# Last keys in a sigmoid attention kernel: products with v issued ahead of the next round's last scores

## Chip, cores and metric

One Trainium2 chip, one core of it. The metric is the device time of one execution in microseconds, as the median of several; lower is better.

## What is computed

Eight batches, twelve heads, 448 positions, head size 64, all in float32; the attention is followed by a feed-forward layer.

```python
scores = scale * np.matmul(q, k.transpose(0, 1, 3, 2)) - np.log(S)    # q, k, v: 8 x 12 x 448 x 64
attn = 1.0 / (1.0 + np.exp(-scores))                                  # a sigmoid, no sum over the keys
attn_out = np.matmul(attn, v)
x = attn_out.transpose(0, 2, 1, 3).reshape(B * S, H * D)              # 3584 x 768
h = x @ w_in                                                          # w_in 768 x 2048
out = np.maximum(0.01 * h, h) @ w_out                                 # w_out 2048 x 768
```

## The kernel before

The kernel has three stages: the attention, the first product of the feed-forward layer (accumulators named f) and the second (accumulators named a). The change touches the attention alone.

A pair is two heads of one batch; there are 48 pairs, and they are worked on two at a time (x and y) in 24 rounds. The 448 keys are cut into four pieces of 128, 128, 128 and 64. For the first three pieces, `scores` makes one score tile each: three products of 64 x 128 array tiles for each of the two heads, in float32 halves (tiles `qks`). The 64 last keys have a score tile of their own for both pairs together, which `last_scores` makes with 64 x 64 array tiles from the raw `qk` tiles, four matmuls, which the trace shows as eight. ScalarE turns every score tile into weights by a sigmoid (`attn`): those of the first pieces into tiles `s`, those of the last keys into room behind a pair's `v` tile, so the trace calls that sigmoid `v<-sc`.

The products with v accumulate in one PSUM tile `pv` for both pairs. `attn_v` adds the first three pieces with 128 x 64 array tiles (twelve instructions a pair), `last_v` adds the last keys with 64 x 64 array tiles (eight instructions). `last_v` reads weights that were made one round earlier: the last scores of a round are computed at the end of the round before it. `Block.keep` then copies `pv` into an `x` tile, on ScalarE, and VectorE adds such tiles up and stores them.

A round is five slots, whose work stands in the list `works` (line 727): both pairs' scores, both pairs' `attn_v`, and `ending`. All matmuls, activations, copies and VectorE operations are pinned to the order in which the code issues them on their engine. ScalarE's order around the boundary of two rounds is therefore: the sigmoid of the last scores (issued within `ending`), the copy `keep` (put at the head of the next slot by `last_v`, with `first=True`), then six sigmoids of the next round's score tiles, in the order x 0, x 1, x 2, y 0, y 1, y 2, then the casts of later inputs.

PSUM is filled by one pool of four buffers (line 688). A round takes eight tiles from it: six score tiles, `pv` and the last scores. A new tile gets the free buffer whose last reader stands earliest in the program. So, in a round: tile x 2 takes the buffer of the last scores (read by the sigmoid `v<-sc`), y 0 that of the round before's `pv` (read by the copy), y 1 that of x 0, y 2 that of x 1, `pv` that of x 2, and the next last scores that of y 0; x 0 and x 1 take those of y 1 and y 2 of the round before. A tile's first weight load waits until the buffer's last reader is done.

Round 0 differs in the order of its first slots, and the last round has no last scores to make: its `last_v` follows `attn_v` directly.

Of the kernel before, what the change touches and what calls it, by code (L numbers as in the profile page):

```python
# [121 lines left out]
def attn_ffn_kernel(ctx: ExitStack, tc: tile.TileContext, qk, v, w_in, w_out, out):  # L122
# [570 lines left out]

    def ending(x, y):

        if y is not None:
            y.last_scores()
        x.last_v()

    unread = psum("s", "unread")[:, 0]  # L700
    for _ in range(IDLE):
# [8 lines left out]
    def when(p, i, jj=0):  # L710
        return base + 2 * (len(PRODUCTS1) * p + i) + jj

    own = {}
    for p in range(NQ):
        for i, n in enumerate(XS):
            if n in XS[:i]:
                continue
            x, t = Own(p, n), when(p, i)
# [6 lines left out]
    for r in range(rounds):  # L725
        x, y, *more = pairs[2 * r:2 * r + 6]
        works = [lambda: whole(x), lambda: whole(y), x.attn_v, y.attn_v, lambda: ending(y, more[0] if more else None)]
        if r == 0:

            works = [works[2], works[1], lambda: None, *works[3:]]  # L730
        if more:
            z, w = more[:2]
            later(0, z.load_v)
            later(1, w.load_v)
            later(2, z.high)
            later(3, z.low, w.high)
            later(4, w.low)
        for n, far in enumerate(more[2:]):
            later(1 + 3 * n, far.load_qk)
        for n, work in enumerate(works):  # L740
            slot(work)
            prepare(ROOM[n] * (r > 0))
# [25 lines left out]
    for g in range(SPLIT1, len(GROUPS1)):  # L768
        for j in range(KQ):
            x = w1[g, j] = Wide(g, j, wb, "wb")  # L770
            prepared_by(base + (g - SPLIT1) * 8 + j, x, 0)
    ws = {}
    for p in range(NQ):
        for n, load in STREAM.items():
            x = ws[p, n] = Streamed(p, n)
# [388 lines left out]
```

## Time and profile before

| what | value |
|---|---|
| median of three runs | 1016.13 us (1015.11 to 1016.46) |
| the profiled execution | 1016.21 us, of which span 1014.4 us |
| TensorE matmul busy | 1008.4 us, 99% of the span |
| VectorE busy | 852.1 us, 84% |
| ScalarE busy | 586.3 us, 58% |
| DMA | 288 GB/s in the mean |

The profile is of one execution. Busy times are those of instructions on an engine; the weight loads of TensorE (PEld) run beside its matmuls. The end of a matmul is a model's value, so a matmul that is shown busy need not be at its peak. A row's "idle before" names what ended an engine's wait, by the semaphore that came last.

### The profile page before, as it was taken

How to read it: one execution, taken by the hardware profiler on the slowest of the kernel's cores; microseconds unless marked ns; L12 is line 12 of the kernel's file. 1: busy time of each engine (PE TensorE's matmuls, PEld its weight loads, DVE VectorE, ACT ScalarE, POOL GpSimd, SP SyncE). 2: the span in 40 equal slices, each digit the busy share in tenths (PEclk: the TensorE clock that was granted, in tenths of full speed). 3: DMA queues.
4: the chain of work that ended last, by engine and by line, in shares of the span. 5: the costliest groups of instructions: out<-in, count | busy, mean ns of one | idle time of the engine just before them, and what ended most of it. 6: DMA issues, size and time to landing. Idle time of an engine off the chain costs nothing.

```text
span 1014.4 us, 15194 instructions
## 1 busy us (share of the span) xinstructions
PE 1008.4 (99%) x5642; PEld 844.0 (83%) x5642; DVE 852.1 (84%) x1116; ACT 586.3 (58%) x710; POOL 0.3 (0%) x5
## 2 busy tenths in 40 slices
PE   9999999999999999999999999999999999999998
PEld 5545555555999999999999999999999999999998
DVE  5888888887898789779788577799998999999886
ACT  7888888887645444445453665465453446645431
POOL 0000000000000000000000000000000000000000
PEclk9999999999999999999999999999999999999999
DMA  9899999997988897899797959996649897775633
GB/s 326 268 339 367 303 371 325 366 333 274 380 303 264 328 326 270 268 356 296 251 328 254 344 197 389 367 327 207 239 145 318 317 384 243 254 259 160 239 110 109
DMA packets 142025, 291.79 MB, mean 288 GB/s; under 512 B 11136, under 2 KB 71680, under 8 KB 141952
## 3 DMA queue, kind: packets, MB, share of 16 engines
q1 hardware_dynamic: 141088, 290.02, 81.9%
q8 instruction: 44, 0.72, 0.3%
q10 hardware_dynamic: 864, 0.80, 0.2%
q14 instruction: 29, 0.24, 0.1%
HBM read 189.33 MB, written 101.45 MB: 287 GB/s over the span
## 4 chain that ended last, share of the span: by engine, by line
PE 92%; DMA 3%; DVE 2%; issue 1%; ACT 1%; SPq 0%; ACTq 0%; DVEq 0%
PE f L159 34%; PE a L159 33%; PE pv L159 13%; PE sc L159 11%; DMA g<-h 1%; DMA g<-g 1%; DMA w<-t 1%; DMA g_m<-g 1%; DVE wd L159 1%; PE e_z L159 0%; DVE h L159 0%; DVE g L159 0%; DVE g_v L159 0%; PE e_a L159 0%; DVE g_m L159 0%
## 5 line engine op out<-in xcount | busy, mean ns | idle before, releaser
L159 PE MATMUL a<-gh,w 128*128 128x448 f32 x1224 | 345.9, 363 | 0.4 <-ACT o L159 0.4
L159 PE MATMUL f<-xh,w 128*128 128x448 f32 x960 | 272.5, 362 | 0.1
L159 PEld LDWEIGHTS a<-gh,w 128*128 128x128 f32 x1224 | 229.7, 188 | 15.6 <-ACT o L159 0.7
L159 PE MATMUL a<-gl,w 128*128 128x448 f32 x540 | 194.5, 360 | 0.4 <-DVE gl L159 0.4
L159 PEld LDWEIGHTS f<-xh,w 128*128 128x128 f32 x960 | 180.0, 187 | 12.8 <-issue 0.7
L159 PE MATMUL f<-xl,w 128*128 128x448 f32 x480 | 173.5, 361 | 0.0
L159 ACT CAST gh<-g 128x896 fp32r<-128x896 f32 x80 | 75.5, 943 | 124.7 <-DVE g L159 102.5
L159 DVE TENSOR_TENSOR h<-h,f 128x896 f32<-128x896 f32 x88 | 95.5, 1086 | 56.5 <-PE f L159 56.4
L159 ACT ACTIVATE s<-sc 128x896 f32<-128x896 f32 x144 | 119.8, 959 | 3.3 <-PE sc L159 3.3
L159 PE MATMUL pv<-s,v 128*64 128x448 f32 x576 | 113.8, 543 | 0.1
L159 PEld LDWEIGHTS a<-gl,w 128*128 128x128 f32 x540 | 101.0, 187 | 8.0 <-DVE gl L159 0.8
L159 ACT COPY h<-f 128x896 f32<-128x896 f32 x56 | 50.1, 909 | 97.4 <-PE f L159 73.7
L159 DVE TENSOR_TENSOR w<-w 128x768 fp32r<-128x768 f32 x112 | 104.3, 951 | 0.9 <-ACT w L159 0.9
L159 PEld LDWEIGHTS sc<-qks 64*128 64x128 f32 x876 | 79.5, 185 | 23.2 <-issue 16.9
L159 ACT CAST w<-w 128x768 fp32r<-128x768 f32 x112 | 92.9, 831 | 6.4 <-DMA w<-t 6.4
L159 PEld LDWEIGHTS f<-xl,w 128*128 128x128 f32 x480 | 90.0, 187 | 6.7
L159 PE MATMUL sc<-qks 64*128 64x448 f32 (+1 forms) x876 | 94.6, 366 | 0.1
L159 PE MATMUL f<-xh,ws 128*128 128x448 f32 x320 | 92.3, 363 | 0.6 <-DVE h L159 0.6
L159 PEld LDWEIGHTS pv<-s,v 128*64 128x64 f32 x576 | 39.2, 137 | 63.2 <-issue 54.0
L159 ACT ACTIVATE h<-h 128x896 f32<-128x896 f32 x56 | 53.2, 953 | 57.8 <-DVE h L159 57.5
L159 DVE TENSOR_TENSOR gl<-g,gh 128x896 fp32r<-128x896 f32 x72 | 78.1, 1085 | 4.4 <-ACT gh L159 3.7
L159 DVE TENSOR_TENSOR xl<-xl,xh 128x896 fp32r<-128x896 f32 x64 | 69.5, 1086 | 12.8 <-ACT xh L159 12.5
(79 smaller groups left out, 1058.7 us busy)
## 6 DMA issues: line engine op xcount, KB each, us to landing
w<-t SPq DMA_DIRECT2D x112, 384.0 KB, 5.1
g<-g SPq DMA_DIRECT2D x81, 448.0 KB, 5.8
xl<-xd SPq DMA_DIRECT2D x64, 448.0 KB, 6.5
g<-h SPq DMA_DIRECT2D x64, 448.0 KB, 5.6
qk<-in_qk SPq DMA_DIRECT2D x46, 448.0 KB, 5.7
xd<-x_s SPq DMA_DIRECT2D x36, 448.0 KB, 6.8
xd<-x SPq DMA_DIRECT2D x28, 448.0 KB, 6.6
wr<-in_w_in SPq DMA_DIRECT2D x24, 512.0 KB, 6.5
```

What stands on the lines that cost most here:

```text
L159: return lambda *args, **kw: tc.keep_in_program_order(issue(*args, **kw))
```

## The change

In `ending`, the two calls change places: y here is the first pair of the next round.

```diff
     def ending(x, y):
 
+        x.last_v()
         if y is not None:
             y.last_scores()
-        x.last_v()
```

No instruction, tile or transfer is added or removed. TensorE does the eight instructions of `last_v` first and then the eight of `last_scores`. On ScalarE the order stays as it was, the sigmoid of the last scores ahead of the copy of `pv`, since the copy is put into the next slot by either order. The order of the PSUM buffers stays too, since it goes by the last readers.

## Rows read from the trace of the kernel before

**Rows 1.** Busy time per engine in stretches; then granted clock, DMA share, GB/s.

```profile
core 0: us, PE busy (x) PEld busy (x) DVE busy (x) ACT busy (x) POOL busy (x), PEclk, DMA share, GB/s
0.00:4.00 4.00, 2.88 (x14) 2.53 (x14) 0.67 (x3) 1.85 (x3) 0.31 (x5) 1.00 0.49 130
...
16.00:250.00 234.00, 234.00 (x1747) 125.67 (x1744) 197.39 (x342) 197.25 (x262) 0.00 (x0) 1.00 0.93 328
250.00:1014.00 764.00, 759.58 (x3790) 709.67 (x3789) 649.56 (x765) 378.89 (x435) 0.00 (x0) 1.00 0.79 275
```

**Rows 2.** TensorE's matmuls in order of time: start us, us, what, count.

```profile
14.57 0.98 PE L159 MATMUL sc<-qk 64*64 64x448 f32 x8
15.37 0.93 PE L159 MATMUL pv<-v 64*64 64x448 f32 x8
16.23 3.91 PE L159 MATMUL sc<-qks 64*128 64x448 f32 x36
...
142.07 4.73 PE L159 MATMUL pv<-s,v 128*64 128x448 f32 x24
146.74 0.98 PE L159 MATMUL sc<-qk 64*64 64x448 f32 x8
147.54 0.93 PE L159 MATMUL pv<-v 64*64 64x448 f32 x8
148.40 3.91 PE L159 MATMUL sc<-qks 64*128 64x448 f32 x36
...
239.90 3.91 PE L159 MATMUL sc<-qks 64*128 64x448 f32 x36
243.74 4.73 PE L159 MATMUL pv<-s,v 128*64 128x448 f32 x24
248.40 0.98 PE L159 MATMUL pv<-v 64*64 64x448 f32 x8
```

**Rows 3.** The chain of waits that ended last, from 120 to 170 us.

```profile
by line: PE pv L159 54.1%; PE sc L159 45.9%
```

**Rows 4.** ScalarE, one instruction each, at the start of one round.

```profile
147.79 0.92 ACT L159 ACTIVATE v<-sc 128x896 f32<-128x896 f32 x1 [2.04 <-PE sc L159]
148.60 0.90 ACT L159 COPY x<-pv 128x896 f32<-128x896 f32 x1
149.39 0.94 ACT L159 ACTIVATE s<-sc 128x896 f32<-128x896 f32 x1
150.19 0.94 ACT L159 ACTIVATE s<-sc 128x896 f32<-128x896 f32 x1
150.99 0.96 ACT L159 ACTIVATE s<-sc 128x896 f32<-128x896 f32 x1
```

**Rows 5.** First weight loads of tiles x 2, y 0, y 1, y 2 and pv.

```profile
149.52 0.19 PEld L159 LDWEIGHTS sc<-qks 64*128 64x128 f32 x2
150.13 0.19 PEld L159 LDWEIGHTS sc<-qks 64*128 64x128 f32 x2
150.74 0.19 PEld L159 LDWEIGHTS sc<-qks 64*128 64x128 f32 x2
151.35 0.19 PEld L159 LDWEIGHTS sc<-qks 64*128 64x128 f32 x2
152.24 0.14 PEld L159 LDWEIGHTS pv<-s,v 128*64 128x64 f32 x2 [0.30 <-ACT s L159]
```

**Rows 6.** Weight loads and matmuls of the round's first score tile.

```profile
148.40 0.19 PEld L159 LDWEIGHTS sc<-qks 64*128 64x128 f32 x2 [0.71 <-issue]
148.51 0.19 PEld L159 LDWEIGHTS sc<-qks 64*128 64x128 f32 x2
...
148.40 0.47 PE L159 MATMUL sc<-qks 64*128 64x448 f32 x2
148.71 0.36 PE L159 MATMUL sc<-qks 64*128 64x448 f32 x2
148.91 0.36 PE L159 MATMUL sc<-qks 64*128 64x448 f32 x2
```

**Rows 7.** Round 0: sigmoids on ScalarE, and weight loads that wait for them.

```profile
11.88 0.91 ACT L159 ACTIVATE s<-sc 128x896 f32<-128x896 f32 x1
12.67 0.93 ACT L159 ACTIVATE s<-sc 128x896 f32<-128x896 f32 x1
...
12.84 0.14 PEld L159 LDWEIGHTS pv<-s,v 128*64 128x64 f32 x2 [0.48 <-ACT s L159]
13.65 0.14 PEld L159 LDWEIGHTS pv<-s,v 128*64 128x64 f32 x2 [0.54 <-ACT s L159]
```

**Rows 8.** ScalarE's sigmoids of the last scores, with the wait before each.

```profile
15.62 0.92 ACT L159 ACTIVATE v<-sc 128x896 f32<-128x896 f32 x1 [0.30 <-PE sc L159]
25.79 0.92 ACT L159 ACTIVATE v<-sc 128x896 f32<-128x896 f32 x1 [2.04 <-PE sc L159]
...
46.12 0.92 ACT L159 ACTIVATE v<-sc 128x896 f32<-128x896 f32 x1 [0.72 <-PE sc L159]
...
239.29 0.92 ACT L159 ACTIVATE v<-sc 128x896 f32<-128x896 f32 x1 [0.66 <-PE sc L159]
```

## Prediction

> **What bounds the kernel now.** I read the busy times by stretch first. Between 16 and 250 us, the attention, TensorE's matmuls cover 234.00 of 234.00 us, and behind it 759.58 of 764 [rows 1]; time is won or lost only where TensorE's stream gets shorter or gets a hole. The chain of waits in the middle of the attention runs through TensorE alone [rows 3]. The matmuls in order of time show a stream that repeats: scores, products with v, last scores, last products with v. From one round's scores to the next it takes 10.17 us, from 16.23 to 239.90 us in 22 such steps, which makes 23 rounds that begin behind an `ending` with last scores in it [rows 2]. The other engine to look at is ScalarE, which reads every score tile and so gives the PSUM buffers back. Over a whole round it has time left: the sigmoid of the last scores finds it idle each time, after 0.30 to 2.04 us of waiting for TensorE [rows 8]. But at the start of a round it works back to back, 0.80 us from start to start [rows 4], while TensorE makes a score tile in 0.61 us (149.52, 150.13, 150.74, 151.35) [rows 5]. For these 4 us ScalarE is the slower of the two, and TensorE runs on because four buffers stand between them. What is to be seen is how much of that lead is left at each tile.
>
> **What moves.** On TensorE the two blocks cost the same in either place. The eight instructions of the last scores begin at 146.74 us and the products 0.80 us later, and the round's scores follow 0.86 us behind [rows 2]. The last round has the products alone right behind `attn_v`, as the change puts them everywhere: they begin 4.66 us after `attn_v`, as the last scores do elsewhere, and take the same 0.98 us [rows 2]. So the new order needs no time of its own: the scores of the round would still begin at 148.40 us. No DMA is moved past another; SP's queue keeps its order, and its transfers start no earlier.
>
> What moves is the moment at which the last scores are ready: their end goes from 147.72 us (146.74 + 0.98) to 148.47 us (147.54 + 0.93), where the products end now. That is 0.75 us later [rows 2]. ScalarE waits for nothing else there [rows 4, 8], so the sigmoid of the last scores starts at 148.54 us in place of 147.79. The copy of `pv` stands behind it. Its data are ready 0.75 us earlier than before, and that is of no use: it is next in line and was already starting back to back. The six sigmoids stand behind the copy. Their scores were complete before they started, so they too are tied to ScalarE's own pace; all of this row of instructions goes 0.75 us later [rows 4].
>
> **Which weight load is late now.** A load that waited for ScalarE began 0.05 us after the sigmoid's end, twice: 11.88 + 0.91 to 12.84, and 12.67 + 0.93 to 13.65 [rows 7]. With that, and with the buffers' order:
>
> - Tile x 2 takes the last scores' buffer: free at 148.71 + 0.75 + 0.05 = 149.51 us, loaded at 149.52 [rows 4, 5]. Just in time. (Today it loads 0.02 us behind the copy's end at 149.50, too soon for a release by the copy; the trace agrees with the buffers' order.)
> - Tile y 0 takes `pv`'s: free at 149.50 + 0.80 = 150.30 us against 150.13: 0.17 late.
> - Tile y 1 takes that of x 0: free at 150.33 + 0.80 = 151.13 against 150.74.
> - Tile y 2 takes that of x 1: free at 151.13 + 0.80 = 151.93 against 151.35.
> - `pv` takes that of x 2: free at 151.95 + 0.80 = 152.75 against 152.24.
>
> What a late load costs lies between two bounds. A load runs beside the matmuls before it: behind an empty array the next load follows the first by 0.11 us, and the first matmul is recorded 0.11 us longer than the others (0.47 against 0.36), while two pairs of matmuls in the stream are 0.20 us apart [rows 6]. So a load can be late by some 0.10 us before its matmul is. With that cover the delays add up to 0.07 at y 0 (0.17 - 0.10), to 0.29 at y 1 (151.13 against 150.81, less 0.10), to 0.48 at y 2 (151.93 against 151.64, less 0.10), and at `pv`, where the load has no cover, to 0.51 (152.75 - 152.24). Without the cover they are 0.17, 0.39 and 0.58, and `pv` follows at 152.82. I take 0.51 us a round, since the first matmul's extra 0.11 us is the same thing seen from the other side, and keep 0.58 as the upper end. The lower end of this case is a release of 0.03 us in place of 0.05, which gives 0.49.
>
> **Is there slack at pv?** The profile gives `pv`'s load an idle time of 0.30 us that a sigmoid ended [rows 5]. But that sigmoid ended at 151.95 us [rows 4], and with 0.05 us it would have let the load go at 152.00. I take the wait until 152.24 to be TensorE's own: three changes of the array's tile size in a round, and the one at 248.40 in the last, all begin 0.06 to 0.07 us before the modelled end of the matmuls ahead (146.80, 148.47, 152.31 and 248.47) [rows 2], with ScalarE done or not. So 0.24 us of slack stand there, and the loss is 0.51 and not 0.75. The Trainium skill, TensorEngine Tiling (Array Packing), Tiling Modes, says that a change of the tiling mode, not of the tile alone, drains the array. By that rule the sum goes by 0.51; by the profile's label it would go by 0.75. The four places agree with the rule.
>
> Behind `pv`, the sigmoids of y are needed only 2 us and more into the products (12 of 24 instructions in 4.66 us) [rows 2], and are done by then. ScalarE's later casts lose nothing, as each round leaves it 0.30 us or more idle [rows 8] and the round gets longer. VectorE's sums of the copied tiles come 0.75 us later, and VectorE is busy 197.39 of 234 us [rows 1]: nothing on TensorE waits for them within a round. So the next round meets the same state, and the loss is paid once a round.
>
> **The sum.** 23 rounds x 0.51 us = 11.7 us. The profiled execution took 1016.21 us (span 1014.4 and 1.8 around it), 0.08 above the median of the runs: 1016.2 + 11.7 = 1027.9, say **1028.0 us**. Its own range is 23 x 0.49 to 23 x 0.58, so 1027.5 to 1029.6.
>
> **The rivals.** A change under 0.2%, 2.0 us, can't be told from none here.
>
> - *Not slower: the lead covers it.* All delays vanish if ScalarE's row moves by less than some 0.24 us, `pv`'s slack: 152.24 - 152.00. That needs the copy to go ahead of the sigmoid on ScalarE, for then the copy starts at 147.79 us, the sigmoid at 148.60, x 0 at 149.39 as today, and x 2 gets its buffer at 149.57 against 149.52, which the 0.10 us of cover hides. Against it: the sigmoid is issued within `ending` and the copy in the next slot. Time 1016.2. Chance 0.07.
> - *A smaller loss*, 0.1 to 0.45 us a round, if the cover of a load is larger than the rows show and `pv` is released earlier: 1018.5 to 1026.5. Chance 0.05.
> - *Tile x 2 gets `pv`'s buffer* in the new order: free at 150.30 against 149.52, less 0.10 of cover: 0.68 us a round, 15.6 us, 1031.8. The load 0.02 us behind the copy speaks against it for today's order [rows 4, 5]. Chance 0.05.
> - *No slack at `pv`*: the label is right, and all of 0.75 us is paid: 17.3 us, 1033.5. Chance 0.08.
> - *The clock falls.* The holes are 0.5 us in 10.7, and the granted clock is 1.00 (2.4 GHz) in every stretch, also in the first 4 us, where TensorE is busy for 2.88 [rows 1]. A round at half the clock would take up to 10.17 us more [rows 2]; one round alone gives 1038, all 23 some 1262. The Trainium skill, TensorE: Matmul & The Clock Gate, A second HAM failure mode: psum-queue depth-cycling, tells of a kernel whose short idles between groups, from cycling through PSUM, made the clock fall again and again. No stretch here shows it. Chance 0.02.
> - *Faster*: I find no mechanism; TensorE's work stays and nothing it waits for comes earlier. Chance 0.01.
>
> **How the numbers follow.** The forecast has the remaining 0.72. The range must hold 8 in 10: with the forecast's own range widened by 2 us below (part of the smaller loss), and up to the full 0.75 us a round, it holds about 0.85: 1025.5 to 1033.8. Slower by over 0.2%: 0.72 + 0.05 + 0.05 + 0.08 + 0.02 = 0.92; within: 0.07; faster: 0.01.
>
> **What the profile after would show.** The round's period 10.68 us in place of 10.17, with the start of the attention's blocks unchanged within `ending`; ScalarE's sigmoid of the last scores 0.75 us later against the round's first scores, and its copy and sigmoids with it; weight loads of y 0, y 1 and y 2 that now wait for ScalarE, and `pv`'s load 0.05 us behind the end of the sigmoid of x 2. The feed-forward stages should look as before, 11.7 us later. The forecast is wrong if those loads don't wait, if the copy is ahead of the sigmoid, or if the clock is below 1.00 anywhere.

## The result, and the profile after

The changed kernel takes 1028.43 us as the median of four runs (1027.49 to 1028.62), against 1016.00 for the kernel before: a ratio of 1.0120, with a 95% interval of 1.0107 to 1.0133. It is 1.2% slower. The forecast was 1028.0 us, with a range of 1025.5 to 1033.8. The profiled execution took 1027.49 us, its span 1025.7. The ratios here and below are those on record, over undisturbed executions, so they are not quite the quotients of the medians; one of the ten executions of the kernel before beside the last experiment took 2057.72 us and counts in the median given there, not in the ratio.

TensorE's matmuls in order of time, the counterpart of [rows 2]:

```profile
16.50 4.43 PE L159 MATMUL sc<-qks 64*128 64x448 f32 x36
...
144.89 4.45 PE L159 MATMUL sc<-qks 64*128 64x448 f32 x36
149.27 4.73 PE L159 MATMUL pv<-s,v 128*64 128x448 f32 x24
153.93 0.98 PE L159 MATMUL pv<-v 64*64 64x448 f32 x8
154.73 0.93 PE L159 MATMUL sc<-qk 64*64 64x448 f32 x8
155.59 4.45 PE L159 MATMUL sc<-qks 64*128 64x448 f32 x36
159.97 4.73 PE L159 MATMUL pv<-s,v 128*64 128x448 f32 x24
...
260.87 0.98 PE L159 MATMUL pv<-v 64*64 64x448 f32 x8
```

A round takes 10.70 us (144.89 to 155.59) in place of 10.17. All of the 0.53 us lies between the first score and the first product: 159.97 - 155.59 = 4.38 us, against 152.24 - 148.40 = 3.84 before, 0.54 with the rounding [rows 2, 5]. The blocks of the last keys keep their lengths and distances: 0.98 and 0.93 us, with 0.80 and 0.86 between the starts.

ScalarE at the start of the same round, one instruction each, the counterpart of [rows 4]:

```profile
155.76 0.92 ACT L159 ACTIVATE v<-sc 128x896 f32<-128x896 f32 x1 [2.58 <-PE sc L159]
156.57 0.90 ACT L159 COPY x<-pv 128x896 f32<-128x896 f32 x1
157.36 0.94 ACT L159 ACTIVATE s<-sc 128x896 f32<-128x896 f32 x1
158.16 0.94 ACT L159 ACTIVATE s<-sc 128x896 f32<-128x896 f32 x1
158.96 0.95 ACT L159 ACTIVATE s<-sc 128x896 f32<-128x896 f32 x1
```

The first weight loads of x 2, y 0, y 1, y 2 and pv, the counterpart of [rows 5]:

```profile
156.73 0.19 PEld L159 LDWEIGHTS sc<-qks 64*128 64x128 f32 x2
157.53 0.19 PEld L159 LDWEIGHTS sc<-qks 64*128 64x128 f32 x2 [0.22 <-ACT x L159]
...
158.35 0.19 PEld L159 LDWEIGHTS sc<-qks 64*128 64x128 f32 x2 [0.32 <-ACT s L159]
159.16 0.19 PEld L159 LDWEIGHTS sc<-qks 64*128 64x128 f32 x2 [0.31 <-ACT s L159]
159.97 0.14 PEld L159 LDWEIGHTS pv<-s,v 128*64 128x64 f32 x2 [0.31 <-ACT s L159]
```

Read the two fences together. The five loads begin 0.05 to 0.06 us behind the ends of the five instructions of ScalarE, one behind the other: 156.68 and 156.73, 157.47 and 157.53, 158.30 and 158.35, 159.10 and 159.16, 159.91 and 159.97. ScalarE's pace of 0.80 us has become the pace of the score tiles. The sum over the attention, in the view of who waited for whom (TensorE's weight loads, 16 to 262 us: total, times, longest):

```profile
PEld sc L159 <- ACT s L159: 14.4, 46, 0.3
PEld pv L159 <- ACT s L159: 7.1, 23, 0.3
PEld sc L159 <- ACT x L159: 4.9, 23, 0.2
```

The counts are 23 and twice 23: one wait for the copy, two for sigmoids ahead of scores and one ahead of products, in each of 23 rounds. In the kernel before, the same view (20 to 262 us) has of these three the line of `pv` alone:

```profile
PEld pv L159 <- ACT s L159: 6.9, 23, 0.3
```

So the waits add up to more than the 12.2 us that were lost: those at `pv` were there before, at no cost to the period, and a late load is partly covered by the matmuls ahead of it. (The view after the change also names a cast of ScalarE for 18 waits of 0.23 us each within the products; the loads beside them, which waited for nothing that the profile shows, stood as long.) TensorE's share of busy time shows nothing of the loss (busy time in stretches, as in [rows 1]):

```profile
16.00:262.00 246.00, 246.00 (x1749) 119.77 (x1742) 196.92 (x340) 197.51 (x262) 0.00 (x0) 1.00 0.90 311
```

TensorE is "busy" for 246.00 of 246 us, in a stage that has become 12 us longer. A matmul that waits for its weights is recorded longer: the 828 instructions of the scores between 16 and 262 us take 385 ns in the mean and 102.0 us of busy time, against 368 ns and 90.0 us before, 12.0 of the 12.2 us lost. So the hole is to be looked for in the weight loads and in the period.

The profiled execution's span grew by 1025.7 - 1014.4 = 11.3 us. The last products with v start 260.87 - 248.40 = 12.47 us later, of which 0.27 arise ahead of the first full round (16.50 against 16.23) and 12.2 = 23 x 0.53 in the rounds. By the end 1.2 us of it had come back: the first product of the feed-forward layer took 0.2 us more, the second 1.4 us less (section on the steps, below).

### The profile page after: what moved, and what is told of

Same layout as the page of the kernel before. It is cut to its first block, busy times and chain, and to the rows that moved or that the text cites. A ratio compares the mean times of both kernels' runs of the same rounds, so it can differ in the third digit from the quotient of the medians.

```text
span 1025.7 us, 15198 instructions
## 1 busy us (share of the span) xinstructions
PE 1020.3 (99%) x5642; PEld 838.6 (82%) x5642; DVE 852.1 (83%) x1116; ACT 586.2 (57%) x710; POOL 0.3 (0%) x5
## 4 chain that ended last, share of the span: by engine, by line
PE 94%; DVE 2%; DMA 1%; issue 1%; ACT 1%; ACTq 0%; DVEq 0%
PE a L159 36%; PE f L159 35%; PE pv L159 12%; PE sc L159 11%; DMA xd<-x_s 1%; DVE wd L159 1%; DMA ws<-ts 1%; PE e_z L159 0%; DVE h L159 0%; DVE ws L159 0%; DVE xl L159 0%; ACT s L159 0%; PE e_a L159 0%; DVE w L159 0%; ACT x L159 0%
## 5 line engine op out<-in xcount | busy, mean ns | idle before, releaser
L159 PEld LDWEIGHTS sc<-qks 64*128 64x128 f32 x876 | 74.1, 184 | 40.7 <-issue 16.9
L159 PE MATMUL sc<-qks 64*128 64x448 f32 (+1 forms) x876 | 106.6, 382 | 0.2 <-ACT qks L159 0.2
L159 DVE TENSOR_TENSOR qks<-qk,qks 128x832 fp32r<-128x832 f32 (+3 forms) x51 | 49.2, 971 | 44.2 <-ACT qks L159 40.0
```

What stands on the lines that cost most here:

```text
L159: return lambda *args, **kw: tc.keep_in_program_order(issue(*args, **kw))
```

## Experiments

### The same order of matmuls, with the copy ahead of the sigmoid on ScalarE

In the changed kernel, `last_scores` issues the sigmoid of the last scores in the next slot, behind the copy of `pv`.

```diff
-            self.last = self.attn(NK - 1, ps, pairs[self.i + 1].room)
+            def weights():
+                self.last = self.attn(NK - 1, ps, pairs[self.i + 1].room)
+
+            later(1, weights, first=True)
```

> The new order of the matmuls is kept, but the sigmoid of the last scores is issued behind the copy of pv instead of ahead of it. Theory (ScalarE's row starts 0.75 us late, because the copy stands behind a sigmoid whose scores come last now): the copy starts where the sigmoid started before, all later sigmoids are back at their old places against the round's scores, no weight load of a score tile waits, period 10.17 us, 1016.2 us (1015.2 to 1017.2). Rival (the matmuls' new order itself costs TensorE 0.5 us a round, whatever ScalarE does): it stays at 1028 us with a period of 10.7 us.

Measured: 1015.08 us against 1015.33 of the kernel before on the same chip, ratio 0.9994 (0.9985 to 1.0004). Its matmuls and ScalarE's instructions:

```profile
144.42 4.73 PE L159 MATMUL pv<-s,v 128*64 128x448 f32 x24
149.08 0.98 PE L159 MATMUL pv<-v 64*64 64x448 f32 x8
149.89 0.93 PE L159 MATMUL sc<-qk 64*64 64x448 f32 x8
150.75 3.91 PE L159 MATMUL sc<-qks 64*128 64x448 f32 x36
154.59 4.73 PE L159 MATMUL pv<-s,v 128*64 128x448 f32 x24
...
150.13 0.91 ACT L159 COPY x<-pv 128x896 f32<-128x896 f32 x1 [2.04 <-PE pv L159]
150.94 0.93 ACT L159 ACTIVATE v<-sc 128x896 f32<-128x896 f32 x1
151.75 0.93 ACT L159 ACTIVATE s<-sc 128x896 f32<-128x896 f32 x1
```

The matmuls stand in the new order, and the period is 10.17 us again (144.42 to 154.59). The copy starts 0.07 us behind the modelled end of the products, 0.62 us ahead of the round's first score (150.13 against 150.75), where the sigmoid stood before (147.79 against 148.40). The first of the six sigmoids comes 1.00 us behind that score, against 0.99 before and 1.77 in the changed kernel. So the order of the matmuls costs nothing of itself; what costs is an order on ScalarE that no longer fits it. Nor does the new order bring anything: TensorE's stream is as long as before. The edit probably does one thing more: tile x 2's first load, at 151.87 us, begins just as the sigmoid of the last scores ends (150.94 + 0.93), with none of the 0.05 us of a release, so x 2 seems to have `pv`'s buffer here, which the copy freed, and y 0 that of the last scores. Neither tile waits, and the doses below, whose buffers keep their order, make the loss without it.

### Three doses of delay on ScalarE, with the matmuls in the order of before

In the kernel before, ScalarE copies the first columns of `pv` once more, into room behind a v tile that nothing else uses. The dose is the number of columns: 2 x 64, 2 x 208 and 2 x 416.

```diff
-            later(1, lambda: block.keep(x.both), first=True)
+            later(1, lambda: block.keep(x.both, x.room), first=True)
...
-        def keep(self, pv):
+        def keep(self, pv, room):
             xs[self.name] = grab(f"x_{self.p}_{self.name}", F32)
             copy(out=xs[self.name], in_=pv[:, :, :S])
+            copy(out=room[:, :, :64], in_=pv[:, :, :64])
```

> The matmuls' order of before; ScalarE copies the first 2 x 64 columns of pv a second time, into unused room, right behind the copy, which puts the six sigmoids about 0.21 us later (estimate from casts of 128 columns that start 0.21 us before the next). Theory: the slack at pv is 0.24 us and the loads have 0.10 us of cover, so nothing is lost: 1016.2 us (1015.2 to 1017.2). Rival (no slack at pv, the profile's label is right): 23 x 0.21 = 4.8 us, 1021.0 us.

> As the dose of 128 columns, with 2 x 208 columns copied a second time, about 0.44 us. Theory: 0.44 - 0.24 = 0.20 us a round, 4.6 us, 1020.7 us (1019.5 to 1022). Rival (no slack at pv): 23 x 0.44 = 10.1 us, 1026 us.

> As the dose of 128 columns, with 2 x 416 columns copied a second time, about 0.78 us: ScalarE's row is as late as in the changed kernel, with the matmuls in the order of before. Theory: 0.78 - 0.24 = 0.54 us a round, 12.4 us, 1028.5 us (1027 to 1030), and weight loads of y 0, y 1 and y 2 that wait for ScalarE. Rival (no slack at pv): 18 us, 1034 us. Rival (the order of the matmuls is what costs): 1016 us.

ScalarE at the start of one round, for the doses of 128, 416 and 832 columns (the round's first weight load begins at 150.87, 153.38 and 155.49 us):

```profile
151.90 0.28 ACT L159 COPY v<-pv 128x128 f32<-128x128 f32 x1
152.06 0.95 ACT L159 ACTIVATE s<-sc 128x896 f32<-128x896 f32 x1
```

```profile
154.42 0.52 ACT L159 COPY v<-pv 128x416 f32<-128x416 f32 x1
154.81 0.95 ACT L159 ACTIVATE s<-sc 128x896 f32<-128x896 f32 x1
```

```profile
156.53 0.88 ACT L159 COPY v<-pv 128x832 f32<-128x832 f32 x1
157.27 0.95 ACT L159 ACTIVATE s<-sc 128x896 f32<-128x896 f32 x1
```

| kernel | first sigmoid behind the first load, us | later than before, us | less 0.24 us of slack | period, us | lost a round, us | ratio to before (95%) |
|---|---|---|---|---|---|---|
| before | 0.99 | | | 10.17 | | |
| dose 128 | 1.19 | 0.20 | 0 | 10.17 | 0.01 | 1.0004 (0.9996 to 1.0013) |
| dose 416 | 1.43 | 0.44 | 0.20 | 10.38 | 0.21 | 1.0047 (1.0033 to 1.0060) |
| dose 832 | 1.78 | 0.79 | 0.55 | 10.73 | 0.56 | 1.0121 (1.0107 to 1.0135) |
| changed kernel | 1.77 | 0.78 | 0.54 | 10.70 | 0.53 | 1.0120 (1.0107 to 1.0133) |

The period of the first dose is that of 22 rounds (18.59 to 242.43 us); single ones were 10.16 to 10.19. The others are those between two starts of the products with v.

The four rows lie on one line: a delay of 0.20 us costs next to nothing, and the other three cost 0.23 to 0.25 us a round less than their delay. So beyond some 0.24 us every further 0.1 us costs 0.1 us a round. The dose of 832 columns does with the old order of the matmuls what the change does with the new one, and its loads wait in the same places. Weight loads of the dose of 832, where "ACT v" is the second copy, now the last reader of `pv`:

```profile
157.45 0.50 PEld L159 LDWEIGHTS sc<-qks 64*128 64x128 f32 x6 [0.24 <-ACT v L159]
158.28 0.51 PEld L159 LDWEIGHTS sc<-qks 64*128 64x128 f32 x6 [0.32 <-ACT s L159]
159.08 0.50 PEld L159 LDWEIGHTS sc<-qks 64*128 64x128 f32 x6 [0.30 <-ACT s L159]
159.89 0.20 PEld L159 LDWEIGHTS pv<-s,v 128*64 128x64 f32 x4 [0.31 <-ACT s L159]
```

Two loads run out of slack almost together. In the kernel before, y 2's load begins 0.17 us behind its release (151.35 against 150.19 + 0.94 + 0.05 us), `pv`'s 0.24 us behind its own. The dose of 128 columns delays ScalarE by 0.20 us: y 2's load is 0.05 us late there (153.87 us, 3.00 behind the round's first load, against 2.95 before), and `pv`'s only 0.01 (154.72 us, 3.85 against 3.84). So a late load is covered, and with the forecast's 0.10 us of cover y 2 would cost time from 0.27 us on. `pv`'s 0.24 us lies within the 0.23 to 0.25 of the table; the two limits are too close for the doses to do more than favour it.

The rival without slack at `pv` is excluded: it wanted 1021, 1026 and 1034 us, and the medians are 1016.33, 1020.50 and 1028.16, against 1015.33 for the kernel before in the same call.

### The new order, with the copy on VectorE

```diff
-            copy(out=xs[self.name], in_=pv[:, :, :S])
+            vcopy(out=xs[self.name], in_=pv[:, :, :S])
```

> The new order of the matmuls, with the copy of pv on VectorE in place of ScalarE. Theory: one item of some 0.80 us falls out of ScalarE's row at the start of a round, so its six sigmoids start 0.02 us earlier than before against the round's scores, although the sigmoid of the last scores comes 0.75 us late; no weight load of y 1, y 2 or pv waits for ScalarE, and the period is 10.17 us if VectorE frees pv's buffer by the load of y 0 (1.7 us behind the round's first load): 1016 us (1015 to 1017.5). Where VectorE, which has 36 us left of 234 and gets 23 more copies of about 1 us, is late with copies or with the inputs' low halves, some of that comes back, up to 1020 us. Rival (the matmuls' new order itself costs): 1028 us or more.

Measured: 1019.03 us against 1016.09, ratio 1.0030 (1.0017 to 1.0043). In a round in which VectorE is in time:

```profile
26.55 1.09 DVE L159 COPY x<-pv 128x896 f32<-128x896 f32 x1 [0.16 <-PE pv L159]
27.17 3.91 PE L159 MATMUL sc<-qks 64*128 64x448 f32 x36
27.33 0.92 ACT L159 ACTIVATE v<-sc 128x896 f32<-128x896 f32 x1 [2.89 <-PE sc L159]
28.15 4.96 ACT L159 ACTIVATE s<-sc 128x896 f32<-128x896 f32 x6
31.01 4.73 PE L159 MATMUL pv<-s,v 128*64 128x448 f32 x24
```

ScalarE's six sigmoids start 0.98 us behind the first score, though the sigmoid ahead of them is still late, and the scores take 3.84 us (27.17 to 31.01), as before. So it is enough to take one item of 0.80 us out of ScalarE's row. That held in 15 of the 23 rounds; the time was expected at 1015 to 1017.5 us, with up to 1020 if VectorE were late with copies. In eight rounds it is late, as it works through other things in its own order (who waited for whom among the weight loads):

```profile
PEld sc L159 <- DVE x L159: 4.7, 8, 0.9
```

One of the eight:

```profile
47.50 1.11 PEld L159 LDWEIGHTS sc<-qks 64*128 64x128 f32 x12 [0.71 <-issue]
48.03 1.08 DVE L159 COPY x<-pv 128x896 f32<-128x896 f32 x1
49.16 2.33 PEld L159 LDWEIGHTS sc<-qks 64*128 64x128 f32 x24 [0.56 <-DVE x L159]
```

The load that waits is the 13th of the round, in all eight. A tile has six, so it is tile x 2 and not y 0: here x 2 has `pv`'s buffer, and the expectation had the wrong tile. That matters, since x 2's load is due 1.12 us behind the round's first load and y 0's 1.73. The eight late loads begin 1.39 to 2.00 us behind; had they been y 0's, one alone would have been late by more than 0.02 us (an estimate from these times; no run has that order of the buffers with the copy on VectorE).

The eight rounds lose 0.18 to 0.79 us each, 4.0 us together, and the attention of this execution is 4.1 us longer than in the profile before (236.23 against 232.17 us from the first full round to the last products with v). The 3 us of the medians need not be the same, as executions also differ at their start and in the second product (below). So the wait moved to another engine, and it comes in 8 rounds of 23, not in all.

## The prediction, step by step

- *The blocks cost the same in either place, and TensorE's stream is all that counts*: right. With the copy ahead of the sigmoid, the new order runs at the old period.
- *ScalarE's row 0.75 us late*: the right mechanism, a little small. It is 0.78 us: the sigmoid of the last scores starts 0.17 us behind the round's first score (155.76 against 155.59), where it started 0.61 ahead of it (147.79 against 148.40). The forecast moved it by the modelled ends of the matmuls, which gave 148.54 against 148.40, so 0.14 behind.
- *Each load 0.05 us behind its reader's end, in the buffers' order given*: right, in all five places (0.05 to 0.06 us). Tile x 2, forecast as just in time, is 0.05 us behind its release too; its load comes 1.14 us behind the round's first load, against 1.12 before.
- *Some 0.10 us of cover for a late load*: right as far as the trace shows it. Tile y 0's load is 0.21 us late (157.53; 1.73 behind the round's first load, as before, would be 157.32). Read as in [rows 6], the load that follows it shows when its first matmul really began: 157.63 in place of 157.52, so 0.11 late. Tile y 2 shows the cover without that reading: its load is 0.62 us late (3.57 behind the first load, against 2.95), and the products behind it only 0.54, so at least 0.08 was covered.

```profile
157.63 0.19 PEld L159 LDWEIGHTS sc<-qks 64*128 64x128 f32 x2
```

- *0.24 us of slack at `pv`, because the wait there is TensorE's own and not ScalarE's*: the slack is right, and it is the step that decided between 0.51 and 0.75. The doses show some 0.24 us of it, though y 2's limit of 0.27 lies close by. The profile's label at that load, a sigmoid, did not name what held it before the change, and after it agrees with the times: the load then stands 0.06 us behind the sigmoid's end, where it stood 0.29 behind. The forecast's sign for a wait of TensorE's own, a start 0.06 to 0.07 us ahead of the modelled end of the matmuls before, does not tell the two apart: it stands in the changed kernel too, where the load follows the sigmoid (159.97 against 155.59 + 4.45 = 160.04). So that the wait was TensorE's own is inferred from the dose of 0.20 us, at which ScalarE was late and next to nothing was lost. That agrees with the Trainium skill, TensorEngine Tiling (Array Packing), Tiling Modes, by which a change of mode drains the array; no run here measured the drain by itself.
- *23 rounds x 0.51 us = 11.7 us*: measured 23 x 0.53 = 12.2 us. ScalarE's delay, forecast 0.03 us too small, accounts for the difference.
- *Feed-forward stages as before*: nearly. The first product starts at 249.31 and now at 261.79 us and the second at 635.16 and 647.83, so the first takes 385.85 and 386.04 us. The second takes 375.9 and 374.6 us to TensorE's last matmul. In it, TensorE waited twice in the kernel before, and not in the changed one (who waited for whom, matmuls, 262 us to the end, kernel before):

```profile
PE a L159 <- DVE gl L159: 0.4, 1, 0.4
PE a L159 <- ACT o L159: 0.4, 1, 0.4
```

The same two waits stand in the profile with the copy ahead of the sigmoid (0.5 and 0.4 us), and not in those of the three doses, whose matmuls have the old order, nor in that with the copy on VectorE. So they don't go with the order of the matmuls. Whether they go with a kernel or with an execution stays open; about 1.4 us of a profiled time goes with them (the second product takes 375.9 us in the two profiles that have them and 374.6 in the five others).
- *The rivals.* The lead that covers it: it exists, but ends at 0.24 us, and the copy did not go ahead of the sigmoid; where it was made to, the time was that of before, as this rival had it. Tile x 2 in `pv`'s buffer: no, its load follows the sigmoid's end. No slack at `pv`: no. A smaller loss, 0.1 to 0.45 us a round: no, it was 0.53. Faster: no. The clock: 1.00 (2.4 GHz) throughout the attention, so holes of half a microsecond did not bring it down here.

## What to carry to other kernels

When two pieces of work change places on one engine, look at the queue of the engine that reads them: an in-order reader whose first item becomes ready last holds up everything behind it, and here the order of two instructions on ScalarE had to change with that of the matmuls. A lead can be measured in slack per buffer: for each buffer, when the reader gives it back against when the writer wants it; the smallest of these, with a late load's cover added where there is one, is what may be spent for nothing (0.24 us here, at `pv`, ahead of 0.17 + 0.10 at y 2), and beyond it every delay is paid in full. An edit can also change which tile gets which buffer, so that is to be read from the new trace too. A label in a profile names what came last by a semaphore; whether it is what held the engine is seen by how long ago it had ended.

## What was not expected of the hardware

The first matmuls of the attention take different times in different executions. Rows of the kernel before, and then of the new order with the copy ahead of the sigmoid, from 4 us:

```profile
4.05 2.53 PE L159 MATMUL sc<-qks 64*128 64x224 f32 x30
```

```profile
4.06 4.07 PE L159 MATMUL sc<-qks 64*128 64x224 f32 x30 [0.16 <-ACT qks L159]
```

The same 30 instructions take 2.53 us in one execution and 4.07 in another, with a granted clock of 1.00 (2.4 GHz) in the profile's rows of both. The first full round begins at 16.23 us in the one and at 18.58 in the other; the doses of 128 and 416 columns began late as well, the dose of 832 and the changed kernel did not, so it does not go with the order of the matmuls. So 2 us of a single time can come from there: the profiled execution with the copy ahead of the sigmoid took 1018.33 us, the longest of its twelve, and the 23 runs of the kernel before beside the first four experiments go from 1014.60 to 1018.54 us. What sets it was not looked into.
